# Third-block gathers and transposes of at least 72 rows in a retention and mixture-of-experts kernel

## The chip, the cores and the metric

The kernel runs on one core of one Trainium2 chip. The metric is the device time of one execution in microseconds. The kernel before has a median of 412.96 us over three runs (410.44 to 413.53).

## The reference

The first half is causal retention over q, k and v of shape (8 batches, 8 heads, 576 positions, 64): scores are q times k transposed, scaled and multiplied by a decay of gamma to the power of the distance, and then multiplied by v. Its result, put side by side over the heads, is x, with 4608 tokens of 512 numbers. The second half is a mixture of eight experts on x:

```python
do_compute = x @ w_skip > 0
logits = xc @ w_gate                      # xc: the tokens with do_compute
e_idx = np.argmax(logits, axis=1)
gate_w = probs[np.arange(len(xc)), e_idx] # softmax of the logits at e_idx
for e in range(8):
    h = np.maximum(xc[mask] @ w1[e], 0.0) # 512 -> 1024
    y[mask] = gate_w[mask, None] * (h @ w2[e])   # 1024 -> 512
out[do_compute] = xc + y                  # other tokens: out = x
```

So each token goes to one expert at most, and an expert works on the rows of x that chose it.

## The kernel before

**Retention stage.** A loop over 36 tiles of 128 tokens computes x and writes it to `out` in DRAM; beside it, the routing gives every token an expert and a slot within that expert. Nothing that the change touches runs here.

**Expert stage.** The experts are ranked by their number of tokens, and the expert of rank e gets a fixed number of slots, `CAPS = (368, 344, 332, 308, 304, 286, 278, 276)`. `blocks(e)` (L480) cuts them into three blocks of at most 128 rows: two full ones and a third with 112, 88, 76, 52, 48, 30, 22 or 20 rows. In this text "expert e" is the one of rank e.

For every expert the work goes through these steps:

- `gather_next` (L1009) calls `gather` (L946), which issues three indirect DMAs on GpSimd's queue through `fetch` (L402). Each brings the rows of `out` that `gidx` lists into one block of `xg`, a tile of 128 partitions by 3 blocks by 512 columns with three buffers. Expert e+1's rows are asked for at the first step of expert e (L1052).
- `turn` (L950) transposes one column chunk of 128 of the three blocks on TensorE (L957) into one PSUM bank `pt`: the rows of `xg` are the stationary operand and an identity of as many rows and columns as the block has is the moving one. `split` (L165) then copies `pt` into `xhi` on ScalarE (L166) and puts the rest into `xlo` on VectorE (L167). An expert has four such chunks; for experts 2 to 7 they stand in steps 3, 4, 5 and 6 of the expert before (L1046), between the two product groups of the step.
- Each expert has eight steps f, one for each 128 columns of the hidden layer. A step does `up` (12 matmuls into `ph`, L488 by way of `three`), then whatever was put between, then `down` of the step before (12 matmuls into `py`). Each matmul of an expert streams all its slots at once, so 308 columns for expert 3.
- The weights of a step come in one 512 KB load `w` on SP's queue (L146), five steps ahead, and are split by ScalarE (`whi_w`) and VectorE (`wlo_w`) on L159. Four buffers hold `w`, six each hold `whi_w` and `wlo_w`.
- `finish` (L986) transposes the result back, multiplies by the gate, adds the token's own row from `xg` (L995) and scatters it with an indirect DMA on GpSimd's queue (L996). It reads only the rows of `blocks(e)`.

TensorE's instructions run in the order in which the program is written (a manual schedule). Expert 0's rows are fetched elsewhere (L395 and L447) and are transposed with `ident` too, its third block of 112 rows through `turn` (L1100). A last loop (L1131) for tokens beyond the slots calls `turn` with one block of 128 rows.

Of the kernel before, what the change touches and what calls it, by code (L numbers as in the profile page):

```python
# [23 lines left out]
P = 128  # L24
# [32 lines left out]
KCUT = 3  # L57
KRANK = 4
CUT = 2 * P
EARLY = ("s", "xt0", "xt1", "sc0", "sc1")  # L60
NCUT = 5

# [3 lines left out]
def kernel(  # L66
# [98 lines left out]
    def split(hi, lo, x):  # L165
        nc.scalar.copy(hi, x)  # L166
        nc.vector.tensor_tensor(lo, x, hi.bitcast(F32), ALU.subtract)  # L167
# [3 lines left out]
    def vec(name, *args, **kw):  # L171
        ins = getattr(nc.vector, name)(*args, **kw)  # L172
        if pinned[0]:
            tc.keep_in_program_order(ins)
        return ins
# [203 lines left out]
    def close_first(ps, nrow):  # L379

        c0 = CNT + NE
        nb = CUT // P
        raw = rt.tile([P, nb, NE, NCMP], F32, tag="raw0", name="raw0", bufs=1)
# [12 lines left out]
        yield 400  # L396
        vec("tensor_scalar", bump, ps[:, c0 : c0 + NE], -1.0, float(CUT), ALU.mult, ALU.add)
        vec("scalar_tensor_tensor", bump, bump, 0.0, lead, ALU.max, ALU.mult)
        yield 400

    def fetch(dst, idx, nrow=NTOK):
        nc.gpsimd.indirect_dma_start(  # L402
            out=dst,
            out_offset=None,
            in_=out[:nrow],
            in_offset=bass.IndirectOffsetOnAxis(ap=idx, axis=0),
            bounds_check=nrow - 1,
            oob_is_err=False,
        )
# [106 lines left out]
    with ExitStack() as actx:  # L516
# [234 lines left out]
        def turn_early(c, tag):  # L751
            pt = pp.tile([P, 2, CUT], F32, tag=tag, name=f"pt_early_{c}")
            for i in range(2):
                for k in range(CUT // P):
                    x = xg0[:, k, (c + i) * P : (c + i + 1) * P]
                    last = nc.tensor.transpose(pt[:, i, k * P : (k + 1) * P], x, ident)
            hi = xhi0[:, c : c + 2, :CUT]
            tc.keep_in_program_order(nc.scalar.copy(hi, pt))
            vec("tensor_tensor", xlo0[:, c : c + 2, :CUT], pt, hi.bitcast(F32), ALU.subtract)
            return last  # L760

        def up_early(f):

            ph = pp.tile([P, 512], F32, tag=EARLY[f], name=f"ph_early_{f}")
            hs[0, f] = [ep.tile([P, CAP], F32R, tag=f"{x}_{f}", name=f"{x}_0_{f}") for x in ("hhi", "hlo")]
            up(ph, blocks(0)[: CUT // P], (xhi0, xlo0), wq[0, f], hs[0, f])
# [75 lines left out]
        for g in range(NT):  # L842
# [22 lines left out]
            if g == NT - 2:  # L865
                hi, lo, t = pieces[0][:3]
# [30 lines left out]
        for f in range(2, NCUT):  # L897
            up_early(f)
        assert not work and not pieces and len(EARLY) == NCUT

# [3 lines left out]
    def bank(tag, name, bufs=1):  # L904
        return (pm if tag == "m" else mpp).tile([P, 512], F32, tag=tag, name=name, bufs=bufs)
# [39 lines left out]

    def gather(e, xg, ks):  # L946
        for k, n in ks:
            fetch(xg[:n, k, :], gidx[:n, k, e : e + 1])

    def turn(e, xg, hi, lo, ks, cs, tag):  # L950

        c0, c1 = ks[0][0] * P, ks[-1][0] * P + ks[-1][1]
        w = c1 - c0
        pt = bank(tag, f"pt_{e}_{cs[0]}_{c0}")[:, : len(cs) * w].rearrange("p (c i) -> p c i", i=w)
        for i, c in enumerate(cs):
            for k, n in ks:
                nc.tensor.transpose(  # L957
                    pt[:, i, k * P - c0 : k * P - c0 + n], xg[:n, k, c * P : (c + 1) * P], ident[:n, :n]
                )
        split(hi[:, cs[0] : cs[-1] + 1, c0:c1], lo[:, cs[0] : cs[-1] + 1, c0:c1], pt)  # L960

    def down(e, f, ks, py, h, w):
        if e == 0:
# [45 lines left out]
    def gather_next(e, xg):  # L1009

        xg[e] = mp.tile([P, NBLK, DM], F32, tag="xg", name=f"xg_{e}", bufs=3)
        gather(e, xg[e], blocks(e))
# [5 lines left out]
    def experts(acts):  # L1018
# [24 lines left out]
        def turn_next(e):  # L1043
            xT[e] = [mp.tile([P, NCC, CAP], F32R, tag=x, name=f"{x}_{e}") for x in ("xhi", "xlo")]
            for c in range(NCC):
                where = ((5, 0), (6, 0), (6, 1), (7, 0))[c] if e == 1 else (3 + c, 0)  # L1046
                at(e - 1, *where, lambda c=c: turn(e, xg[e], *xT[e], blocks(e), [c], ("pt", "m")[c % 2]))
# [5 lines left out]
        for n in range(len(steps) + 1):  # L1053
# [35 lines left out]
            if last and last[2] is late:  # L1089
                for f in range(NCUT):  # L1090
                    down(0, f, late, py[0], hs[0, f], wq[0, f])
                split_raw(len(raw))
            elif last:
                e, f, ks = last
                if e not in py:
                    py[e] = [bank(f"py{c}", f"py_{e}_{c}") for c in range(NBLK if e == 0 else NCC)]
                if n == NCUT:
                    down(e, f, ks[:1], py[e], hs[e, f], wq[e, f])
                    for cs, tag in (((0, 1), "pt"), ((2, 3), "py3")):
                        turn(0, xg0, xhi0, xlo0, late, cs, tag)  # L1100
                    ks = ks[1:]
                down(e, f, ks, py[e], hs[e, f], wq[e, f])
                if f == NFC - 1:
                    y = evacuate(e, py[e])
                    if e + 1 < NE:
                        for k, where in zip(blocks(e), ((1, 1), (2, 0), (2, 1))):
                            at(e + 1, *where, finish, e, y, xg[e], [k])
                    else:
                        finish(e, y, xg[e], blocks(e), ("pt", "m", "ph"))
# [21 lines left out]
    with tc.For_i(0, nblock, 1):  # L1131
# [28 lines left out]
        for c in range(NCC):  # L1160
            turn(0, xg0, xhi0, xlo0, one, [c], ("pt", "py3")[c % 2])
# [71 lines left out]
```

## Time and profile before

| what | value |
|---|---|
| median of three runs | 412.96 us (410.44 to 413.53) |
| the profiled execution's own time | 413.26 us |
| its span, first to last instruction | 411.6 us |
| mean granted TensorE clock | 0.994 |
| TensorE matmuls (PE) busy | 393.9 us, 96% |
| TensorE weight loads (PEld) busy | 354.8 us, 86% |
| VectorE, ScalarE, GpSimd busy | 256.4, 152.8, 115.9 us |
| moved by DMA | 91.54 MB |

The span is the profiled execution without what lies before its first and after its last instruction, here 1.7 us. PE and PEld are two lanes of one engine: the load of the next stationary operand can run while a matmul streams, so their shares add up to more than the whole. A row of the timeline gives the start, the length and the engine of an instruction; several like ones in a row are merged and counted with x. Matmuls overlap in such rows, since their ends are modelled: the distance from one start to the next tells what one costs. A row of the groups gives, behind the first bar, busy time and mean length in ns of one, and behind the second the idle time of the engine just before them. The word "issue" in a wait says that the engine stood still and that no semaphore of the profile explains it.

### The profile page before, as it was taken

To read this page: it belongs to the slowest core of one execution; us is meant where nothing else is said; L and a number is where in the kernel's file an instruction comes from. 1 tells how busy PE (TensorE), PEld (TensorE's weight loads), DVE (VectorE), ACT (ScalarE), POOL (GpSimd) and SP (SyncE) were. 2 spreads that over 40 slices of the span, in tenths; PEclk is the share of its full clock that TensorE was granted. 3 is DMA by queue.
4 is the path that set the end of the run, shared out by engine and by line. 5 is a ranking of instruction groups with operands and counts; after the bars stand their busy time and mean duration, and the time that the engine had idled before them with its cause. 6 is when DMAs were issued, how large, how long until landed. Compare 5 with 4: busy or idle time off the path is not lost.

```text
span 411.6 us, 11862 instructions
## 1 busy us (share of the span) xinstructions
PE 393.9 (96%) x4905; PEld 354.8 (86%) x4905; DVE 256.4 (62%) x569; ACT 152.8 (37%) x264; POOL 115.9 (28%) x138
## 2 busy tenths in 40 slices
PE   8989998998999999999999999999999999999991
PEld 4768778887878779879999999999999999999990
DVE  3655776685598768787455646955655645655522
ACT  2222322231334343164444344445445445445210
POOL 6523322222335550701500430240240330400402
PEclk9999999999999999999999999999999999999997
DMA  8999998999999482656644563555555664642101
GB/s 310 408 358 314 376 352 283 361 375 346 338 399 384 191 236 74 209 168 262 197 163 153 158 211 117 180 169 179 174 174 178 200 188 164 206 134 97 55 0 56
DMA packets 28733, 91.54 MB, mean 222 GB/s; under 512 B 4090, under 2 KB 4218, under 8 KB 28676
## 3 DMA queue, kind: packets, MB, share of 16 engines
q1 hardware_dynamic: 19584, 71.31, 50.4%
q0 software_dynamic: 3616, 9.86, 6.9%
q10 hardware_dynamic: 5476, 9.57, 6.1%
q8 instruction: 40, 0.66, 0.7%
q14 instruction: 17, 0.14, 0.1%
HBM read 76.54 MB, written 14.55 MB: 221 GB/s over the span
## 4 chain that ended last, share of the span: by engine, by line
PE 57%; DMA 21%; issue 13%; POOL 4%; DVE 3%; ACT 1%; ACTq 0%; POOLq 0%
DMA out<-rs,sidx 15%; PE py L488 12%; PE ph L488 10%; PE pxt L664 8%; PE psc L594 6%; DMA xg<-out,gidx 5%; PE px L715 5%; PE pxt L685 4%; PE ps_s L644 4%; POOL out L996 2%; PE pl L724 2%; PE ph_early L488 2%; POOL xg L402 1%; DMA tt_sb<-ttab 1%; DVE sc L172 1%
## 5 line engine op out<-in xcount | busy, mean ns | idle before, releaser
L159 DVE TENSOR_TENSOR wlo_w<-w,whi_w 128x1024 fp32r<-128x1024 f32 x59 | 71.9, 1223 | 62.6 <-ACT whi_w L159 62.6
L159 ACT CAST whi_w<-w 128x1024 fp32r<-128x1024 f32 x59 | 61.6, 1050 | 61.6 <-PE py L488 60.1
L996 POOL DMA_INDIRECT out<-rs,sidx x24 | 32.8, 1367 | 155.6 <-DVE rs L995 152.4
L488 PE MATMUL py<-hhi,whi_w 128*128 128x344 f32 (+6 forms) x224 | 70.6, 315 | 0.0
L488 PE MATMUL ph<-xhi,whi_w 128*128 128x344 f32 (+6 forms) x224 | 68.9, 307 | 0.0
L488 PE MATMUL ph<-xhi,wlo_w 128*128 128x344 f32 (+6 forms) x224 | 67.9, 303 | 0.0
L488 PE MATMUL ph<-xlo,whi_w 128*128 128x344 f32 (+6 forms) x224 | 67.7, 302 | 0.0
L488 PE MATMUL py<-hlo,whi_w 128*128 128x344 f32 (+6 forms) x224 | 67.7, 302 | 0.0
L488 PE MATMUL py<-hhi,wlo_w 128*128 128x344 f32 (+6 forms) x224 | 67.6, 302 | 0.0
L629 POOL TENSOR_TENSOR v<-v,tt_sb 128x512 f32<-128x512 f32 x36 | 38.7, 1074 | 89.9 <-DVE xt L172 62.3
L717 ACT COPY xn<-px 128x512 f32<-128x512 f32 x36 | 21.1, 587 | 83.3 <-PE px L715 77.1
L172 DVE TENSOR_TENSOR sc<-psc,mask 128x512 f32<-128x512 f32 x72 | 46.3, 685 | 8.6 <-PE psc L594 4.5
L172 DVE TENSOR_TENSOR xt<-pxt,gt_sb 128x256 f32<-128x256 f32 x72 | 27.2, 419 | 35.3 <-PE pxt L685 32.0
L496 ACT ACTIVATE hhi<-ph 128x344 fp32r<-128x344 f32 (+7 forms) x59 | 25.2, 428 | 57.3 <-PE ph L488 57.3
L488 PEld LDWEIGHTS py<-hhi,whi_w 128*128 128x128 f32 x224 | 42.2, 188 | 0.9
L488 PEld LDWEIGHTS ph<-xhi,whi_w 128*128 128x128 f32 x224 | 42.2, 189 | 0.2
L488 PEld LDWEIGHTS ph<-xlo,whi_w 128*128 128x128 f32 x224 | 42.2, 189 | 0.1
L488 PEld LDWEIGHTS py<-hlo,whi_w 128*128 128x128 f32 x224 | 42.2, 189 | 0.0
L488 PEld LDWEIGHTS ph<-xhi,wlo_w 128*128 128x128 f32 x224 | 42.2, 188 | 0.0
L488 PEld LDWEIGHTS py<-hhi,wlo_w 128*128 128x128 f32 x224 | 42.2, 188 | 0.0
L664 PE MATMUL pxt<-sc,v 128*64 128x128 f32 x576 | 39.4, 275 | 0.3 <-DVE sc L172 0.3
L497 DVE SCALAR_TENSOR_TENSOR hlo<-ph,hhi 128x344 fp32r<-128x344 f32 (+7 forms) x59 | 28.1, 476 | 15.2 <-ACT hhi L496 14.2
(185 smaller groups left out, 595.5 us busy)
## 6 DMA issues: line engine op xcount, KB each, us to landing
w<-w SPq DMA_DIRECT2D x64, 512.0 KB, 3.8
q<-qkv SPq DMA_DIRECT2D x36, 512.0 KB, 6.0
v<-qkv SPq DMA_DIRECT2D x36, 512.0 KB, 6.2
out<-xn ACTq DMA_DIRECT2D x36, 256.0 KB, 6.0
out<-rs,sidx POOLq DMA_INDIRECT x24, 3.8
xg<-out,gidx POOLq DMA_INDIRECT x21, 5.1
wg_sb<-wg ACTq DMA_DIRECT2D x1, 64.0 KB, 6.4
tt_sb<-ttab ACTq DMA_DIRECT2D x1, 56.0 KB, 5.3
```

Of the source, the lines that this page charges most:

```text
L159: both = nc.scalar.copy(hi, t), nc.vector.tensor_tensor(lo, t, hi.bitcast(F32), ALU.subtract)
L172: ins = getattr(nc.vector, name)(*args, **kw)
L488: nc.tensor.matmul(ps, x, y, start=first and n == 0, stop=last and n == 3 * len(terms) - 1)
L496: nc.scalar.activation(hi, ph, AF.Relu)
L497: nc.vector.scalar_tensor_tensor(lo, ph, 0.0, hi.bitcast(F32), ALU.max, ALU.subtract)
L594: nc.tensor.matmul(psc[r][halves[c], a, k0:], q[halves[r], 1, a, k0 : k0 + D], q[halves[r], 0, a, k0:], start=a == 0, stop=a == NPR - 1, s ...
L629: ins = nc.gpsimd.tensor_tensor(v, v, vt_sb[:, place(g), :].unsqueeze(2).broadcast_to([P, H, D]), ALU.mult)
L644: nc.tensor.matmul(ps_s[halves[r], a, :], k[:, head(a, r), :], v[:, head(a, r), :], start=t in (0, NPD // 2) and a == 0, stop=a == NPR - 1 ...
L664: nc.tensor.matmul(pxt[a % 2][halves[j], a // 2, :], v[:, head(a, r), :], sc[:, r, a, :], start=a < 2, stop=t == 0 and a >= NPR - 2, skip_ ...
L715: nc.tensor.transpose(px[:, c * P : (c + 1) * P], xt_t[b][:, c, o * P : (o + 1) * P], ident)
L717: moved = nc.scalar.copy(xn, px)
L996: put = nc.gpsimd.indirect_dma_start(out=out, out_offset=bass.IndirectOffsetOnAxis(ap=sidx[:n, k, e : e + 1], axis=0), in_=rs[:n], in_offs ...
```

## The change

A constant of 72 rows is added. `gather` and `turn` use it as the least number of rows of a block; blocks of more rows stay as they are. The bank `pt` is laid out with the padded width, and `split` reads only the columns that belong to the expert. The slots beyond the expert's own still have an index (of some token, or 0), so the additional rows are rows of `out`; nothing reads their transposed columns.

```diff
+ROWS = 72
...
     def gather(e, xg, ks):
         for k, n in ks:
+            n = max(n, ROWS)
             fetch(xg[:n, k, :], gidx[:n, k, e : e + 1])
 
     def turn(e, xg, hi, lo, ks, cs, tag):
 
         c0, c1 = ks[0][0] * P, ks[-1][0] * P + ks[-1][1]
-        w = c1 - c0
+        ks = [(k, max(n, ROWS)) for k, n in ks]
+        w = ks[-1][0] * P + ks[-1][1] - c0
         pt = bank(tag, f"pt_{e}_{cs[0]}_{c0}")[:, : len(cs) * w].rearrange("p (c i) -> p c i", i=w)
...
-        split(hi[:, cs[0] : cs[-1] + 1, c0:c1], lo[:, cs[0] : cs[-1] + 1, c0:c1], pt)
+        split(hi[:, cs[0] : cs[-1] + 1, c0:c1], lo[:, cs[0] : cs[-1] + 1, c0:c1], pt[:, :, : c1 - c0])
```

The third blocks of experts 3 to 7 grow from 52, 48, 30, 22 and 20 rows to 72. Each of them is gathered once and transposed in four chunks, so the change touches 5 indirect DMAs and 20 transposes. Nothing else differs in what the engines are given, and no instruction changes its place. One of the 20 places, on TensorE, is expert 4's first chunk, in step 3 of expert 3 (`xg` is the gathered tile, `pt` the bank, `ph` and `py` the products around it). Before:

```order
L488 MATMUL ph_3_0_4254<-xlo_3876,whi_w_3_3977_3979 128x308
L488 MATMUL ph_3_0_4254<-xhi_3875,wlo_w_3_3977_3980 128x308
L957 MATMUL pt_0_0_4271<-ident,xg_4115 128x128 x2
L957 MATMUL pt_0_0_4271<-ident,xg_4115 128x48
L488 MATMUL py_0_4165<-hhi_2_4197,whi_w_2_3936_3938 128x308
L488 MATMUL py_0_4165<-hlo_2_4198,whi_w_2_3936_3938 128x308
```

And with the change, where every line stands three (in the products: one) further down:

```order
L489 MATMUL ph_3_0_4254<-xlo_3876,whi_w_3_3977_3979 128x308
L489 MATMUL ph_3_0_4254<-xhi_3875,wlo_w_3_3977_3980 128x308
L960 MATMUL pt_0_0_4271<-ident,xg_4115 128x128 x2
L960 MATMUL pt_0_0_4271<-ident,xg_4115 128x72
L489 MATMUL py_0_4165<-hhi_2_4197,whi_w_2_3936_3938 128x308
L489 MATMUL py_0_4165<-hlo_2_4198,whi_w_2_3936_3938 128x308
```

The third transpose has 72 columns (and 72 rows of `xg`) in place of 48; the products around it are the same and stand where they stood.

## The prediction

> **What bounds the kernel now.** I read the page's first part, then a table by stretches, then who waited for whom, and at last the timeline around the instructions that change. The page:
>
> ```profile
> span 411.6 us, 11862 instructions
> PE 393.9 (96%) x4905; PEld 354.8 (86%) x4905; DVE 256.4 (62%) x569; ACT 152.8 (37%) x264; POOL 115.9 (28%) x138
> ```
>
> TensorE is the busy engine, and its weight loads run beside its matmuls (96% and 86% of one span). That is a mean over two stages, so the expert stage is looked at by itself. The stretches are: expert 1's steps (which turn expert 2's 76-row block), the stretch that holds all 20 changed places, what follows, and the tail. The columns are length, busy time and count of PE, PEld, DVE, ACT and POOL, granted clock, DMA share and GB/s:
>
> ```profile
> 200.00:235.00 35.00, 35.00 (x234) 34.88 (x233) 19.39 (x27) 15.19 (x23) 6.50 (x6) 1.00 0.51 164
> 235.00:369.00 134.00, 134.00 (x954) 129.43 (x954) 80.94 (x137) 62.08 (x99) 32.72 (x25) 1.00 0.54 176
> 369.00:383.00 14.00, 14.00 (x112) 14.00 (x112) 9.05 (x15) 6.72 (x11) 1.72 (x1) 1.00 0.24 77
> 383.00:411.60 28.60, 19.55 (x154) 18.82 (x152) 7.34 (x13) 3.84 (x8) 5.48 (x5) 0.92 0.10 40
> ```
>
> From 235 to 369 us PE shows a matmul in flight at every moment, at the full clock, while VectorE works 60% of the time and ScalarE 46%. The weight loads alone stand still for 134.00 - 129.43 = 4.57 us there, and before that stretch for only 0.12 us of 35. The waits of the weight loads and of ScalarE in 235 to 383 and 235 to 369 us (time in total, times, longest):
>
> ```profile
> PEld pt L957 <- issue: 3.3, 20, 0.2
> ```
>
> ```profile
> ACT whi_w L159 <- PE py L488: 40.0, 31, 1.6
> ```
>
> TensorE waits for no other engine in this stretch; its one row is 20 stops of "issue" ahead of L957, which no semaphore ends. In turn the weights' casts wait for TensorE to free a buffer (40.0 us), and no row there has them wait for a load. So **TensorE is the bound, and the others have slack**: what is cut from its line of work shortens the end.
>
> Where the 20 stops lie, the groups of weight loads by shape tell (busy, mean ns, then the idle time before):
>
> ```profile
> L957 PEld LDWEIGHTS pt<-ident,xg 128*128 128x128 f32 x48 | 6.6, 141 | 0.1
> L957 PEld LDWEIGHTS pt<-ident,xg 76*128 76x128 f32 x4 | 0.6, 140 | 0.0
> L957 PEld LDWEIGHTS pt<-ident,xg 52*128 52x128 f32 x4 | 0.5, 134 | 0.7 <-issue 0.7
> L957 PEld LDWEIGHTS pt<-ident,xg 48*128 48x128 f32 x4 | 0.5, 134 | 0.7 <-issue 0.7
> L957 PEld LDWEIGHTS pt<-ident,xg 20*128 20x128 f32 x4 | 0.5, 134 | 0.7 <-issue 0.7
> L957 PEld LDWEIGHTS pt<-ident,xg 22*128 22x128 f32 x4 | 0.5, 134 | 0.7 <-issue 0.7
> L957 PEld LDWEIGHTS pt<-ident,xg 30*128 30x128 f32 x4 | 0.5, 133 | 0.7 <-issue 0.7
> ```
>
> Loads of 128 and of 76 rows follow without a stop. Loads of 52 rows and fewer stop for about 0.17 us each, and 52 rows stop as long as 20. So it isn't a cost per row; something changes between 52 and 76 rows.
>
> **The change part by part.** *The transposes* of 20 blocks go to 72 rows. A group is two transposes of 128 rows and one short one, and then a product. Since ends are modelled, I take starts: from the first transpose to the second product behind the group (the first product's own start is also affected), less one product's pitch (second to third product). The timeline of TensorE, first for two of expert 2's four groups, with 76 rows:
>
> ```profile
> 202.78 0.45 PE L957 MATMUL pt<-ident,xg 128*128 128x128 f32 x3
> ...
> 203.26 0.32 PE L488 MATMUL py<-hlo,whi_w 128*128 128x344 f32 x1
> 203.42 0.32 PE L488 MATMUL py<-hhi,wlo_w 128*128 128x344 f32 x1
> ...
> 215.12 0.45 PE L957 MATMUL pt<-ident,xg 128*128 128x128 f32 x3
> ...
> 215.61 0.32 PE L488 MATMUL py<-hlo,whi_w 128*128 128x344 f32 x1
> 215.76 0.32 PE L488 MATMUL py<-hhi,wlo_w 128*128 128x344 f32 x1
> ```
>
> 0.48 - 0.16 = 0.32 and 0.49 - 0.15 = 0.34: 0.33 us for a group without a stop. Then the first group of experts 3, 4, 5, 6 and 7, with 52, 48, 30, 22 and 20 rows:
>
> ```profile
> 235.30 0.57 PE L957 MATMUL pt<-ident,xg 128*128 128x128 f32 x3
> ...
> 236.07 0.31 PE L488 MATMUL py<-hlo,whi_w 128*128 128x332 f32 x1
> 236.22 0.32 PE L488 MATMUL py<-hhi,wlo_w 128*128 128x332 f32 x1
> ...
> 267.67 0.57 PE L957 MATMUL pt<-ident,xg 128*128 128x128 f32 x3
> ...
> 268.42 0.30 PE L488 MATMUL py<-hlo,whi_w 128*128 128x308 f32 x1
> 268.56 0.31 PE L488 MATMUL py<-hhi,wlo_w 128*128 128x308 f32 x1
> ...
> 298.51 0.55 PE L957 MATMUL pt<-ident,xg 128*128 128x128 f32 x3
> ...
> 299.24 0.31 PE L488 MATMUL py<-hlo,whi_w 128*128 128x304 f32 x1
> 299.39 0.30 PE L488 MATMUL py<-hhi,wlo_w 128*128 128x304 f32 x1
> ...
> 328.55 0.55 PE L957 MATMUL pt<-ident,xg 128*128 128x128 f32 x3
> ...
> 329.26 0.29 PE L488 MATMUL py<-hlo,whi_w 128*128 128x286 f32 x1
> 329.39 0.29 PE L488 MATMUL py<-hhi,wlo_w 128*128 128x286 f32 x1
> ...
> 357.30 0.55 PE L957 MATMUL pt<-ident,xg 128*128 128x128 f32 x3
> ...
> 358.01 0.29 PE L488 MATMUL py<-hlo,whi_w 128*128 128x278 f32 x1
> 358.14 0.29 PE L488 MATMUL py<-hhi,wlo_w 128*128 128x278 f32 x1
> ```
>
> - expert 3: 0.77 - 0.15 = 0.62 us
> - expert 4: 0.75 - 0.14 = 0.61
> - expert 5: 0.73 - 0.15 = 0.58
> - expert 6: 0.71 - 0.13 = 0.58
> - expert 7: 0.71 - 0.13 = 0.58
>
> The trace has no 72-row transpose. Its cost is bounded by the two nearest shapes: 0.33 us a group as with 76 rows, 0.62 as with 52. I take 0.33: 72 is 4 rows from the one and 20 from the other, and columns matter little, since 52 of them cost 0.04 us more than 20 do. The gain per group is 0.29, 0.28, 0.25, 0.25 and 0.25 us, 1.32 us for one group of each expert, and with four groups each **5.3 us**. The 3.3 us of stops ahead of the short loads are part of it; the other 2.0 us lie behind the short transpose, where the next product starts late too.
>
> By the Trainium skill (TensorEngine Tiling (Array Packing), section "Key Properties") the engine drains when its tiling mode changes, and its configurations have 128, 64 or 32 rows; 72 rows would be in the mode of the products, and no drain would be left, which gives the same sum and puts the step at 64 rows.
>
> *The gathers* carry 20, 24, 42, 50 and 52 more rows, 188 in all. A row has 512 numbers of 4 bytes, so that is 385 KB more. None of the five is late. The last one is the tightest, from the chain of waits:
>
> ```profile
> 336.44 5.57 DMA xg<-out,gidx
> ...
> 342.08 10.71 issue
> ...
> 353.02 1.76 POOL out L996
> ```
>
> It lands at 342.01 us and is first read at 357.30, 15.3 us later; for 72 rows to come late, the landing would have to take 20.9 us in place of 5.57. GpSimd's instructions stay 3 for each expert, in the same places, and those of this line took between 0.95 and 1.78 us with no order by rows:
>
> ```profile
> L402 POOL DMA_INDIRECT xg<-out,gidx x21: 948/1069/1784, 166.8 to 336.4; - x21
> ```
>
> I put the issue at nothing: GpSimd is busy 32.72 us of 134, and the scatter queued behind these gathers starts only at 353.02. The bytes are put at nothing as well, since the casts of the weights wait for TensorE and not for loads; if that cover were gone, 385 KB at the stretch's 176 GB/s would cost 2.2 us at most, and less than nothing is excluded, as no byte is saved.
>
> *The split* reads as many columns as before from a wider bank: nothing. VectorE and ScalarE have to do the same work in 129 us rather than 134, which makes 63% and 48%.
>
> **Sum.** 413.26 us of the profiled execution less 5.3 gives 408.0. This execution lies 0.3 us above the median of the runs shown, 412.96, so as a median I expect **407.7 us**. A measurement of this kernel tells about 1% from no change, 4.1 us; the bound for faster is therefore 408.8.
>
> **Rivals.**
>
> *No change, 413.0 us.* The step lies between 72 and 76 rows, or short loads stop for another reason than their rows, such as being the last before a product of other tiles. For it: 72 is not in the trace. Against it: expert 2's 76-row block stands in the same place in the same order and doesn't stop. The mechanism would be that a load can't pass a matmul that uses the same rows of the array; then padding takes away what could overlap. But in 369 to 383 us the loads are busy all 14.00 us beside matmuls that are busy all 14.00, and all of them have 128 rows, so full loads do pass. The Trainium skill (TensorE: Matmul & The Clock Gate, section "Part 3: Packing small matmuls — row/col tiling") has such a rule: a load overlaps matmuls in flight only when its row groups differ. By that rule the padded load would stop as well, and this rival's time would stand; the rows above speak against it.
>
> *Part of it, 409.7 us.* Only the stops ahead of the load go (3.3 us), and what lies behind the short transpose belongs to the change from transposes to products. Against it: expert 2's groups have both parts short.
>
> *Given back to the DMA, 409.9 us.* The loads of `w` share the queues' engines with 385 KB more, and TensorE, now faster, waits for weights: 5.3 - 2.2 = 3.1 us are left. It decides from the point where casts wait for `w` in place of `py`. Against it stands the 40.0 us row.
>
> *Slower by the clock.* TensorE without its stops could be granted less. From 235 to 369 us 128.7 us of work are left, so below a clock of 0.96 (128.7/134) the gain is gone; at the 0.92 of the tail it would be 128.7/0.92 - 128.7 = 11.2 us more, 412.96 - 5.3 + 11.2 = 418.9 us. Against it: the clock was 1.00 in 369 to 383 us, where no load stops at all, and 0.92 only where TensorE idles.
>
> **How the numbers follow.** The forecast has a chance of 0.80, no change 0.07, part of it 0.05, given back 0.05, slower 0.03. The runs before lie between 2.5 below their median and 0.6 above it. I put the range at 405.6 to 410.2: below, the forecast less 2.1 for such a spread; above, it takes in the two cases of 409.7 and 409.9 and leaves out no change and slower, and a little of the forecast. The forecast is only 1.1 us under the bound of 1%, so I count nine tenths of it as faster: 0.72. The rest of it and three rivals are the same: 0.08 + 0.07 + 0.05 + 0.05 = 0.25. Slower is 0.03.
>
> **What would show it.** In the profile after, the 20 transposes of 72 rows have no "issue" before their loads, the 3.3 us row is gone, a group takes 0.33 us by the same reckoning, and PEld is busy nearly all of the stretch. The gathers land 5 to 6 us after issue as before, and the casts still wait for `py`. I am wrong if the 72-row loads stop like those of 52 rows, if `whi_w` waits for `w`, or if the clock in the stretch falls under 1.00.

## The result, and the profile after

The changed kernel has a median of 407.03 us over four runs (405.39 to 408.05), against 413.16 us (410.44 to 413.53) for four runs of the kernel before (one more than the three of the table ahead). The ratio is 0.988, with a 95% interval of 0.983 to 0.993: faster, by about 1.2%. The forecast was 407.7 us in a range of 405.6 to 410.2, so the median lies within it. A later repetition (below) gave 0.985 (0.981 to 0.990).

The page of the profiled execution, which took 406.93 us by itself:

```profile
span 405.2 us, 11862 instructions
PE 388.5 (96%) x4905; PEld 354.0 (87%) x4905; DVE 256.2 (63%) x569; ACT 151.1 (37%) x264; POOL 113.9 (28%) x138
```

The same 4905 matmuls and 4905 weight loads, and about as many microseconds of loads as before, but PE is busy 5.4 us less. By stretches, from expert 1's steps on (columns as in the prediction; the second stretch holds 19 of the 20 changed places, since expert 3's first group now starts at 233.89 us, in the first stretch):

```profile
200.00:235.00 35.00, 35.00 (x235) 34.87 (x234) 20.15 (x28) 15.47 (x25) 7.68 (x6) 1.00 0.52 165
235.00:364.00 129.00, 129.00 (x957) 128.65 (x957) 80.73 (x138) 60.19 (x98) 29.79 (x25) 1.00 0.57 184
364.00:377.00 13.00, 13.00 (x105) 12.96 (x105) 8.54 (x12) 6.36 (x11) 1.85 (x2) 1.00 0.23 80
```

954 matmuls took 134 us in the prediction's stretch of 235 to 369 us; now 957, nearly the same ones, take 129. The weight loads stand still for 0.35 us there and not for 4.57, and the granted clock is still 1.00. VectorE works 63% of the time and ScalarE 47%. The weight loads of the transposes by shape, and the wait of ScalarE that is the longest in total in 235 to 364 us:

```profile
L960 PEld LDWEIGHTS pt<-ident,xg 128*128 128x128 f32 x48 | 6.6, 141 | 0.1
L960 PEld LDWEIGHTS pt<-ident,xg 72*128 72x128 f32 x20 | 2.8, 140 | 0.0
L960 PEld LDWEIGHTS pt<-ident,xg 76*128 76x128 f32 x4 | 0.6, 140 | 0.0
```

```profile
ACT whi_w L160 <- PE py L489: 37.7, 32, 1.6
```

All 20 loads of 72 rows come without a stop, and the waits of PEld show no row from 200 to 383 us, where there was one of 3.3 us. The casts of the weights still wait for TensorE to free a buffer, so the loads of `w` keep ahead. The timeline around a group, first of expert 4's in the second stretch and then of expert 7's:

```profile
265.08 0.45 PE L960 MATMUL pt<-ident,xg 128*128 128x128 f32 x3
265.33 0.39 PE L489 MATMUL py<-hhi,whi_w 128*128 128x308 f32 x1
265.56 0.30 PE L489 MATMUL py<-hlo,whi_w 128*128 128x308 f32 x1
265.70 0.31 PE L489 MATMUL py<-hhi,wlo_w 128*128 128x308 f32 x1
...
351.59 0.45 PE L960 MATMUL pt<-ident,xg 128*128 128x128 f32 x3
...
352.05 0.29 PE L489 MATMUL py<-hlo,whi_w 128*128 128x278 f32 x1
352.18 0.29 PE L489 MATMUL py<-hhi,wlo_w 128*128 128x278 f32 x1
```

By the prediction's reckoning a group costs 0.48 - 0.14 = 0.34 us (expert 4, 0.61 before) and 0.46 - 0.13 = 0.33 (expert 7, 0.58 before). Where within the group the time went, the single starts tell, for expert 4's group before and after:

```profile
267.78 0.46 PE L957 MATMUL pt<-ident,xg 128*128 128x128 f32 x2
267.98 0.26 PE L957 MATMUL pt<-ident,xg 48*128 48x48 f32 x1
268.17 0.41 PE L488 MATMUL py<-hhi,whi_w 128*128 128x308 f32 x1
```

```profile
265.19 0.34 PE L960 MATMUL pt<-ident,xg 128*128 128x128 f32 x2
265.30 0.23 PE L960 MATMUL pt<-ident,xg 72*128 72x72 f32 x1
265.33 0.39 PE L489 MATMUL py<-hhi,whi_w 128*128 128x308 f32 x1
```

(Rows of narrow windows, in which the merged ones come apart; the first row of each begins with the second full transpose.) The short transpose started 0.20 us behind the full one and now starts 0.11 behind it; the product started 0.19 us behind the short one and now starts 0.03 behind it.

**A ruler for the experiments.** Whole executions of one kernel differ by some microseconds, so besides the ratio I use the distance within a profile from the first transpose of expert 2's first group to the last product's start. Both lie in the stage in which TensorE never waits, with the 20 places between them. The start before the change is quoted in the prediction, 202.78 us; its end, by the timeline of the kernel before:

```profile
400.63 0.29 PE L488 MATMUL py<-hhi,wlo_w 128*128 128x276 f32 x1
```

And both ends after the change:

```profile
201.37 0.45 PE L960 MATMUL pt<-ident,xg 128*128 128x128 f32 x3
...
393.93 0.29 PE L489 MATMUL py<-hhi,wlo_w 128*128 128x276 f32 x1
```

197.85 us became 192.56: **5.29 us** gained, where the prediction worked out 5.3. The two spans differ by 6.4 us, however. 1.4 us of that (202.78 to 201.37) lie ahead of the first changed place, in code that is the same in both kernels, and are a difference between two executions.

### The profile page after: what moved, and what is told of

Its sections match the earlier page's. It is cut to its first block, busy times and chain, and to the rows that moved or that the text cites. A ratio compares the mean times of both kernels' runs of the same rounds, so it can differ in the third digit from the quotient of the medians.

```text
span 405.2 us, 11862 instructions
## 1 busy us (share of the span) xinstructions
PE 388.5 (96%) x4905; PEld 354.0 (87%) x4905; DVE 256.2 (63%) x569; ACT 151.1 (37%) x264; POOL 113.9 (28%) x138
## 4 chain that ended last, share of the span: by engine, by line
PE 62%; DMA 19%; issue 12%; POOL 3%; DVE 1%; ACT 1%; POOLq 0%; ACTq 0%
DMA out<-rs,sidx 16%; PE py L489 12%; PE ph L489 10%; PE pxt L665 8%; PE psc L595 7%; PE px L716 5%; PE pxt L686 5%; PE ps_s L645 5%; DMA xg<-out,gidx 3%; POOL out L999 2%; PE pl L725 2%; PE ph_early L489 2%; PE ps_m L95 1%; PE pn L740 1%; POOL xg L403 1%
```

## The experiments

The theory: a transpose whose stationary operand has at most 64 rows uses TensorE in another way than the 128-row products around it. It is as if the engine emptied before it and after it, and this costs about 0.27 us for one excursion (out of the 128-row stream and back). The rivals: each short load costs its stop by itself; the cost falls gradually with more rows; the rows that the gathers add cost or gain something. The runs with 64, 65 and 128 rows and with the gathers alone shared one chip and its runs of the kernel before, and the last three runs shared another set.

**64 rows and 65 rows.** To find the step, one constant of the changed kernel:

```diff
-ROWS = 72
+ROWS = 64
```

> The constant is 64 in place of 72. Theory (a load of at most 64 rows takes the array out of the way in which the 128-row products use it, and the engine empties before and after): the 64-row loads stop like those of 52 rows, about 0.17 us each, 3.3 us of stops in all, and a group costs about 0.62 us by the reckoning of the prediction; the time is that of the kernel before within half a per cent, ratio 0.997 to 1.003. Rival (the cost falls gradually with more rows, or 72 is enough only because it is near 76): a group lies between 0.33 and 0.62 us, and the ratio between 0.988 and 0.997.

> The constant is 65, one row more than in the run with 64. Theory (the step is between 64 and 65 rows): no stop is left, a group costs about 0.33 us, and the ratio to the kernel before is that of 72 rows, 0.985 to 0.990. Rival (gradual, or a step higher up): as with 64 rows, or between the two.

With 64 rows the ratio is 0.999 (0.996 to 1.002), with 65 rows 0.985 (0.981 to 0.989). The weight loads by shape and the one wait of PEld, with 64 rows:

```profile
L960 PEld LDWEIGHTS pt<-ident,xg 64*128 64x128 f32 x20 | 2.7, 135 | 3.3 <-issue 3.3
```

```profile
PEld pt L960 <- issue: 3.3, 20, 0.2
```

and with 65 rows, where the waits of PEld show no row at all from 230 to 383 us:

```profile
L960 PEld LDWEIGHTS pt<-ident,xg 65*128 65x128 f32 x20 | 2.8, 140 | 0.0
```

One row and one column more, and all 20 stops are gone. So the step is between 64 and 65, and nothing is gradual. With 64 rows the timeline for expert 4 reads

```profile
267.26 0.58 PE L960 MATMUL pt<-ident,xg 128*128 128x128 f32 x3
...
268.02 0.30 PE L489 MATMUL py<-hlo,whi_w 128*128 128x308 f32 x1
268.16 0.31 PE L489 MATMUL py<-hhi,wlo_w 128*128 128x308 f32 x1
```

0.76 - 0.14 = 0.62 us for a group, a hundredth more than with 48 rows. Expert 7's first group costs 0.62 as well, where it cost 0.58 with 20 rows. So 64 rows are a little slower than the shorter ones before: on the ruler they take 198.38 us (0.53 more than before) and 65 rows 192.58. The rival of a gradual cost is refuted.

**The gathers alone.** The kernel before, with

```diff
     def gather(e, xg, ks):
         for k, n in ks:
+            n = max(n, 72)
             fetch(xg[:n, k, :], gidx[:n, k, e : e + 1])
```

> The kernel before with the gathers alone at 72 rows; the transposes read 52 to 20 rows as before. Theory (all of the gain is on TensorE, the additional 385 KB are hidden): stops of 3.3 us as before, ratio 0.997 to 1.003. Rival (the bytes take back up to 2.2 us): ratio up to 1.005. Rival (the rounder gathers themselves gain something): ratio under 0.997.

The ratio is 1.002 (0.999 to 1.005) and the ruler shows 197.86 us against 197.85. The additional bytes did move, as the queue's row shows (it was 9.86 MB before):

```profile
q0 software_dynamic: 3744, 10.25, 7.3%
```

0.39 MB more, no time that could be measured: the gain doesn't come from the gathers.

**128 rows.** The changed kernel with `ROWS = 128`.

> The constant is 128: experts 1 to 7 gather and transpose full third blocks, 632 rows or 1.29 MB more than the kernel before. Theory (bytes hidden, no stop from 65 rows on): ratio as with 72 rows, 0.985 to 0.990, and a group again costs about 0.33 us, since 76 and 72 columns cost the same. Rival (the bytes cost their time): 1.29 MB at 176 GB/s are 7.4 us, so the gain of 5.3 would be gone and the ratio at or over 1.00.

The expectation counted the rows wrongly: experts 1 to 7 add 560 rows, 1.15 MB (6.5 us at 176 GB/s), not 632. The queue's row and the landing times of the gathers in this run:

```profile
q0 software_dynamic: 3728, 11.01, 7.9%
```

```profile
DMA to landing us min/median/max: 3.4/4.6/6.9
```

1.15 MB more than before, and the gathers land as they did (3.2/4.9/6.8 before). The ratio is 0.988 (0.983 to 0.993) and the ruler shows 192.48 us. Three times the bytes of the change are hidden too, and between 65 and 128 neither rows nor columns count.

**Each short transpose twice.** The kernel before, without padding:

```diff
             for k, n in ks:
+                for _ in range(2 if n <= 64 else 1):
                     nc.tensor.transpose(
```

> The kernel before with each of the 20 short transposes done twice in a row into the same columns. Theory (what costs is the change from 128 rows to at most 64 and back, not the short load as such): the second one follows without a stop, 20 stops and 3.3 us of them stay, a group grows by a transpose's pitch of at most 0.11 us, 2.2 us in all, ratio 1.003 to 1.006. Rival (each short load stops by itself): 40 stops, 6.6 us of them, a group grows by 0.25 to 0.29 us, 5.3 us in all, ratio 1.011 to 1.015.

The ratio is 1.002 (0.999 to 1.005), a little under both expectations, and the ruler 199.07 us, 1.22 more than before or 0.06 for each of the 20 additional transposes. Loads by shape for two of the five shapes, and the wait:

```profile
L958 PEld LDWEIGHTS pt<-ident,xg 52*128 52x128 f32 x8 | 0.8, 138 | 0.7 <-issue 0.7
...
L958 PEld LDWEIGHTS pt<-ident,xg 20*128 20x128 f32 x8 | 0.8, 135 | 0.7 <-issue 0.7
```

```profile
PEld pt L958 <- issue: 3.4, 20, 0.2
```

Twice as many short loads (x8 where x4 stood), and still 20 stops. A second short transpose behind a first one is nearly free: 0.06 us, where the first costs 0.25 to 0.29 more than a padded one. So it isn't the short load that costs, but going over to it and back.

**Two short transposes in a row.** The kernel before, without padding, turning chunks two at a time for experts 3 to 7, at steps 3 and 5:

```diff
+    def turn_two(e, xg, hi, lo, ks, cs):
+        w = CAPS[e]
+        pts = [bank(tag, f"pt_{e}_{c}_0")[:, :w] for c, tag in zip(cs, ("pt", "m"))]
+        for part in (ks[:-1], ks[-1:]):
+            for c, pt in zip(cs, pts):
+                for k, n in part:
+                    nc.tensor.transpose(pt[:, k * P : k * P + n], xg[:n, k, c * P : (c + 1) * P], ident[:n, :n])
...
+            if e > 2:
+                for c in (0, 2):
+                    at(e - 1, 3 + c, 0, lambda c=c: turn_two(e, xg[e], *xT[e], blocks(e), [c, c + 1]))
+                return
```

> The kernel before with the chunks of experts 3 to 7 turned two at a time, into two banks: four transposes of 128 rows, then the two short ones in a row; rows are not padded. Theory (the change of rows costs): 10 stops in place of 20, 1.65 us of them, about half of the 5.3 us is gained, ratio 0.991 to 0.996. Rival (each short load stops): 20 stops as before and ratio 0.998 to 1.002.

The ratio is 0.990 (0.986 to 0.994), just under the 0.991 to 0.996 expected. The wait from 230 to 383 us, and the timeline of one pair for expert 4:

```profile
PEld pt L969 <- issue: 1.7, 10, 0.2
```

```profile
265.08 0.85 PE L969 MATMUL pt<-ident,xg 128*128 128x128 f32 x6
...
266.11 0.30 PE L488 MATMUL py<-hlo,whi_w 128*128 128x308 f32 x1
266.25 0.31 PE L488 MATMUL py<-hhi,wlo_w 128*128 128x308 f32 x1
```

Ten stops in place of 20, with no row padded and no byte added. A pair costs 1.03 - 0.14 = 0.89 us where two single groups cost 2 x 0.61 = 1.22, so 0.33 us are gained for a pair. The ruler shows 194.69 us, 3.16 less than before. That is a little over the half (2.6) that was expected, since a second short transpose adds less (0.06 us, by the run before) than the 0.11 us at which full ones follow each other.

**The change again.**

> The changed kernel once more, unchanged, for a narrower interval beside the two others: ratio 0.985 to 0.990 if the 5.3 us are all of it; 0.982 to 0.985 if there is a second gain beside the 20 groups.

The ratio is 0.985 (0.981 to 0.990), and the ruler shows 192.56 us, as in the first profile. That ratio lies at the edge between the two expectations, but the ruler leaves no second gain: with 65, 72 and 128 rows it is 192.58, 192.56 and 192.48 us.

| kernel | ratio (95% interval) | ruler, us | against before |
|---|---|---|---|
| before | 1 | 197.85 | |
| 72 rows (the change) | 0.988 (0.983 to 0.993) | 192.56 | -5.29 |
| 72 rows again | 0.985 (0.981 to 0.990) | 192.56 | -5.29 |
| 65 rows | 0.985 (0.981 to 0.989) | 192.58 | -5.27 |
| 128 rows | 0.988 (0.983 to 0.993) | 192.48 | -5.37 |
| 64 rows | 0.999 (0.996 to 1.002) | 198.38 | +0.53 |
| gathers alone | 1.002 (0.999 to 1.005) | 197.86 | +0.01 |
| short ones twice | 1.002 (0.999 to 1.005) | 199.07 | +1.22 |
| short ones in pairs | 0.990 (0.986 to 0.994) | 194.69 | -3.16 |

No version is measurably better than the change; 65 rows do the same with the fewest additional rows.

## Why the prediction was right, point by point

- *TensorE is the bound from 235 us on.* Right: the 5.29 us cut from its line came off the end of that line in full, and none of it turned into a wait elsewhere.
- *A 72-row transpose costs what a 76-row one costs.* Right: 0.33 to 0.34 us a group. The bound from above, 0.62 us, would have been the truth with 64 rows.
- *The gain is more than the 3.3 us of stops, since the product behind a short transpose starts late as well.* Right in the sum: the rival that kept only the 3.3 us fails, and in the pairs 3.16 us went with ten stops, 1.7 us of them. The split into 3.3 and 2.0 us isn't borne out. By the starts of the matmuls the short transpose came 0.09 us late (0.20 less 0.11), which is 1.9 us for 20, and the other 3.4 us lay behind it. So of a load's 0.17 us of stop only about half delayed its own transpose.
- *The gathers' bytes are hidden.* Shown by the gathers alone (+0.01 us on the ruler) and, beside the faster TensorE, by 1.15 MB that cost nothing. With 72 rows they land 3.2 to 6.1 us after their issue, 4.6 in the median (3.2 to 6.8 and 4.9 before).
- *The rival that no padded load can pass a matmul on the same rows* is refuted by 65, 72 and 128 rows, whose loads don't stop. In the stretch after, the loads are busy for 128.65 of 129.00 us beside matmuls that are busy all 129.00 (the matmuls' ends are modelled) and that use the same rows. So the rule that the prediction took from the Trainium skill (TensorE: Matmul & The Clock Gate, "Part 3: Packing small matmuls — row/col tiling"), that a load overlaps matmuls in flight only when its row groups differ, doesn't hold for these loads as it stands. The same section also lets a load into the background weight buffer go ahead of matmuls in flight, which fits.
- *The rule of draining* in the Trainium skill (TensorEngine Tiling (Array Packing), "Key Properties") says that a change of the tiling mode drains the engine. All that was measured agrees with it: the step lies between 64 and 65 rows, and the cost comes once for each excursion and not once for each short transpose. The runs show this behaviour and its size, 0.25 to 0.29 us for one excursion; that the engine drains inside is the page's word for it and isn't in any row here, nor is it shown that a transpose takes such a mode from its rows alone.
- *The clock* stayed at 1.00 in the stretch.
- *The time.* The median came out 0.7 us under the forecast, within the range. The mechanism's own term was right to a hundredth or two on the ruler (5.29 against 5.3 us); the medians differ by 6.1 us. What is left is the difference between executions, of which 1.4 us in the two profiles lie ahead of the change. As runs of one kernel lie 3 us and more apart, that the median came so close is in part luck.

One thing the prediction couldn't tell from its groups, and the experiments above don't tell either: rows from columns. A transpose's identity is square, so both change together, from 64 to 65 too. The profile of the kernel before has the answer in its retention stage, where products of 64 rows (L685) follow products of 128 rows (L664). The timeline of PE, and then of the loads:

```profile
33.31 1.04 PE L664 MATMUL pxt<-sc,v 128*64 128x128 f32 x16
34.29 0.67 PE L685 MATMUL pxt<-q,st 64*64 64x128 f32 x16
```

```profile
33.42 0.69 PEld L664 LDWEIGHTS pxt<-sc,v 128*64 128x64 f32 x12
34.28 0.42 PEld L685 LDWEIGHTS pxt<-q,st 64*64 64x64 f32 x16 [0.17 <-issue]
```

Both stream 128 columns here and both have 64 columns of stationary operand; of the shapes only the rows differ, and the first 64-row load stops for the same 0.17 us. It does so at all 32 such places, 28 of them with 128 streamed columns. So a change of rows alone comes with the stop, and ordinary products stop like transposes. That fewer rows are the only cause isn't shown: in the same stage a load of 128 rows and 64 columns stops as well when it follows 128-row loads of 128 columns,

```profile
46.06 0.47 PEld L739 LDWEIGHTS pn<-ident,lt 128*128 128x128 f32 x4
46.70 0.31 PEld L644 LDWEIGHTS ps_s<-v 128*64 128x64 f32 x8 [0.17 <-issue]
```

while the transposes of `finish`, with 20 to 88 such columns, don't:

```profile
L993 PEld LDWEIGHTS yn<-ident,yT 128*52 128x52 f32 x4 | 0.4, 104 | 0.0
```

What makes that difference stays open.

## What to carry to other kernels

A lone transpose with at most 64 rows of stationary operand, in a stream of 128-row products, costs more than a padded one: here 0.25 to 0.29 us each time, for reading 20 to 52 rows and not 72. (Products of 64 rows show the same stop of their first load; what padding them would gain wasn't measured.) Look for it in the profile as weight loads of one shape that stop for "issue" while their neighbours don't. Pad to 65 rows or more where the additional rows are free, or put the short ones next to each other so that one excursion serves several.

## What was not expected of the hardware

The step is as sharp as one row: 64 rows stop 20 times of 20, 65 rows never. Behind a first short transpose the second one starts after 0.08 to 0.11 us, and the product behind it follows sooner than it does behind a single one (for expert 4 after 0.15 us and not 0.19), so 20 additional transposes cost 1.22 us together, 0.06 each, less than the about 0.11 us at which full ones follow each other. And the stops were a small part of a lane that the page of the profile calls 86% busy: it is the groups by shape that showed them, not the shares.
